# A new written order for the first tile of a linear-attention and gated-MLP kernel, on all engines

## The chip, the cores and the metric

The kernel runs on one core of a Trainium2 chip. The metric is the device time of one execution in microseconds. Five engines work in parallel, each through its own instructions in order: TensorE (PE in the profile, its weight loads PEld), VectorE (DVE), ScalarE (ACT), GpSimd (POOL) and SyncE (SP), which here issues all transfers.

## The reference

Inputs are r, k, v of shape (4, 8, 768, 48), a decay w and a bonus u per head and channel, and three MLP weights of 384x1536, 384x1536 and 1536x384, all float32.

```python
for t in range(S):
    cur = np.einsum('bhd,bhe->bhde', u[None] * kt, vt)
    y[:, :, t] = np.einsum('bhd,bhde->bhe', rt, state + cur)
    state = w[None, :, :, None] * state + np.einsum('bhd,bhe->bhde', kt, vt)
...
x = np.ascontiguousarray(attn_out.transpose(0, 2, 1, 3)).reshape(B * S, H * D)
gate = 1.0 / (1.0 + np.exp(-(x @ w_gate)))
val = x @ w_val
return (gate * val @ w_out).astype(np.float32)
```

## The kernel before, in words

The recurrence is computed in 12 chunks of 64 tokens; a chunk has two groups of heads, so there are 24 pieces n = 0, 1, 2, ... (a chunk's group 1 comes before its group 0). Two chunks make a tile of 512 tokens for the MLP; there are six tiles. The MLP's hidden width goes in 12 blocks f of 128. Every fp32 operand of the MLP is split into a high and a low part, and a product is three passes of matmuls (low weights by high x, high by high, high by low).

The first tile is special. The weights still have to be loaded and split while it runs, and its x comes chunk by chunk. So its MLP goes in 14 items i: blocks 0 and 1 for chunk 0 alone (256 columns, items 0 and 1), blocks 0 and 1 for chunk 1 (items 2 and 3), then blocks 2 to 11 for both (512 columns, items 4 to 13). All its work, with the attention of pieces 0 to 7 and part of 8 and 9, is written out by hand in the table START (line 42): 293 steps, run one after another by the loop behind `steps`; every step adds its instructions to the lists of the engines it uses, and each engine then works through its list in that order. Where a step's input isn't there, the engine waits, and everything behind it in its list waits too.

The letters of START that the prediction speaks of (n is a piece, f a block, i an item):

- L.n and X.n load a piece's channel-major tile (chan) and token-major tile (toks), W.f a block's weight words (wr, 1152 KB); all go through SyncE's one queue, in START's order. chan and toks have three buffers each. W.0's words lie in the buffer that W.11 needs.
- tk, ti, tp make the powers of the decay on VectorE; tp also copies them in turned order (line 184), tt transposes that on TensorE, tn writes the table tabn.
- A.n scales keys by the bonus (ScalarE, line 278); R.n scales the queries (line 284; on GpSimd, as Rv on VectorE); k.n scales the keys in place (VectorE, line 295); T.n scales the token-major keys (line 299; Tv on VectorE).
- Z.n makes the scores (TensorE, 64 matmuls, line 366), K.n keeps their causal part (VectorE, line 374), I.n applies them and, from n = 2 on, the state (line 328), O.n makes the outer products for the state. I.n takes two of the three PSUM banks named ring; they come free when h.n and l.n (high and low part of x, lines 465 and 469) and s.n (sum into the state; line 440 copies it for n = 0 and 1, line 438 adds) have read them. d.n decays the state (ScalarE, line 419).
- c.f, j.f, w.f, o.f rebuild and split a block's weights: scale (ScalarE, 232), three integer operations (VectorE, 238 to 240), high part (ScalarE, 246), low part (GpSimd, 249; ov on VectorE). Block 0 goes in two halves, c0, j0, w0, o0.
- U.i is the up product (18 matmuls into two ring banks, line 506), g.i sigmoid, m.i product, H.i and q.i high and low part of h (q on GpSimd, qv on VectorE, line 528), D.i the down product (9 matmuls, line 544). F.n copies x rows by small transfers (line 473).

Behind START a loop treats the other five tiles in a fixed pattern; U.14 is its first step.

Of the kernel before, what the change touches and what calls it, by code (L numbers as in the profile page):

```python
# [39 lines left out]


START = """
L.0 tc A.0 W.0 c0.1 X.1 tk ti.0 ti.1 tp L.1 W.1 Rv.0 k.0 c0.0 X.0 j0.1 Z.0 A.1 X.2 w0.1 j0.0 k.1
K.0 o0.1 I.0 W.2 tt w0.0 c.1 tn j.1 Tv.0 L.2 h.0 R.1 w.1 L.3 c.2 o.1 Tv.1 Z.1 l.0 K.1 A.2 O.0 W.5
s.0 I.1 k.2 O.1 R.2 F.0 X.3 s.1 h.1 A.3 Z.2 o0.0 W.3 X.4 l.1 L.4 K.2 W.7 T.2 U.0 R.3 g.0 k.3 I.2
O.2 c.3 W.4 Z.3 j.2 h.2 d.2 l.2 R.4 m.0 s.2 H.0 F.2 K.3 A.4 j.3 U.1 L.5 g.1 X.5 I.3 w.2 h.3 qv.0
d.3 T.4 T.3 w.3 D.0 k.4 O.3 l.3 R.5 s.3 m.1 Z.4 A.5 U.2 o.2 c.4 g.2 K.4 H.1 I.4 d.4 k.5 O.4 h.4 j.4
X.6 qv.1 Z.5 W.6 w.4 m.2 s.4 H.2 D.1 l.4 o.3 U.3 L.6 L.7 c.5 qv.2 D.2 W.11 g.3 K.5 F.4 o.4 A.6 m.3
j.5 H.3 Tv.5 U.4 g.4 R.6 qv.3 w.5 m.4 W.9 ov.5 F.1 I.5 O.5 H.4 D.3 d.5 h.5 k.6 Z.6 s.5 l.5 A.7 U.5
c.6 F.3 q.4 D.4 g.5 k.7 X.7 j.6 F.5 c.7 m.5 H.5 U.6 T.6 j.7 w.7 K.6 q.5 W.10 D.5 o.7 g.6 w.6 Rv.7  # L50
m.6 H.6 q.6 U.7 c.9 g.7 Z.7 ov.6 I.6 O.6 h.6 d.6 j.9 m.7 D.6 W.8 l.6 s.6 c.8 H.7 w.9 U.8 j.8 q.7
D.7 T.7 g.8 w.8 m.8 o.9 H.8 ov.8 q.8 U.9 g.9 D.8 K.7 U.10 c.10 m.9 c.11 H.9 j.10 g.10 I.7 q.9 m.10
O.7 H.10 h.7 l.7 d.7 w.10 D.9 q.10 s.7 ub L.8 X.8 Y.8 L.9 X.9 Y.9 U.11 D.10 g.11 j.11 m.11 o.10
U.12 F.6 H.11 w.11 g.12 ov.11 q.11 R.8 t.8 k.8 b.8 T.8 i.8 m.12 H.12 D.11 U.13 R.9 t.9 qv.12 k.9
g.13 m.13 H.13 Z.8 K.8 qv.13 b.9 T.9 i.9 D.12 F.7
"""


# [1 line left out]
def rwkv_then_moe(ctx: ExitStack, tc: tile.TileContext, wd, ub, ch, tk, rt, wt, rk0, vn0, wd0, out):  # L60
    nc = tc.nc
# [361 lines left out]

    def add_state(n):
        c, g = GROUPS[n]
        parts = [(0, 0, 0, 112)]
# [1 line left out]
        for s, to, lo, rows in parts:  # L430
# [444 lines left out]
```

## Time and profile before

| what | value |
|---|---|
| median of 3 runs | 558.22 us (557.37 to 559.66) |
| the profiled execution | 559.26 us |
| its span, first to last instruction | 557.5 us |
| TensorE busy | 521.9 us, 94% of the span |
| VectorE, ScalarE, GpSimd busy | 235.4, 184.1, 212.9 us |
| mean granted TensorE clock | 0.986 |

A profile gives busy time by engine, the engines' timelines with the idle time before each row and what ended it, and the same in windows. The clock is given as a share of its upper level: 1.00 is 2.4 GHz, 0.50 is 1.2 GHz. The idle time of an engine that nothing waits for costs nothing.

### The profile page before, as it was taken

The page shows a single profiled execution, that of the slowest core. Times are in us where ns is not written, and L with a number is a line of the kernel's source. Part 1 is how long each engine was busy: PE and PEld are TensorE (multiplying, and loading weights), DVE is VectorE, ACT ScalarE, POOL GpSimd, SP SyncE. Part 2 cuts the span into 40 slices and gives each one's busy share as a digit, 9 for nine tenths or more (in the row PEclk, how much of TensorE's full clock was granted, in tenths as well). Part 3 has the DMA queues.
Part 4 walks back from the last instruction along what each step waited for, and adds up shares of the span by engine and source line. Part 5 has one row for each costly group of instructions (what it writes and reads, how often), then busy time and mean ns, then how long its engine had stood idle before and what let it go on. Part 6 is the DMA issues. An engine that isn't in the chain of part 4 may idle for free. (4 is left out here: it accounts for less than half of the span.)

```text
span 557.5 us, 11987 instructions
## 1 busy us (share of the span) xinstructions
PE 521.9 (94%) x5204; PEld 427.1 (77%) x5204; DVE 235.4 (42%) x364; ACT 184.1 (33%) x394; POOL 212.9 (38%) x165
## 2 busy tenths in 40 slices
PE   1596899999999999999999999999999999999994
PEld 1486778777888888888888888888888888888883
DVE  7798799786524414324414324314324110101001
ACT  4466454633422322422322422322322221221111
POOL 3534234648254424254424254424234121111220
PEclk9998799999999999999999999999999999999998
DMA  8698911040221303221303221303220001100001
GB/s 329 265 364 311 368 36 54 30 111 2 88 83 52 92 16 86 79 77 67 92 15 88 77 80 65 93 13 89 78 75 5 11 1 19 58 0 1 0 1 61
DMA packets 15723, 47.84 MB, mean 86 GB/s; under 512 B 2384, under 2 KB 5200, under 8 KB 14256
## 3 DMA queue, kind: packets, MB, share of 16 engines
q1 hardware_dynamic: 15664, 47.01, 24.7%
q8 instruction: 43, 0.70, 0.5%
q14 instruction: 16, 0.13, 0.1%
HBM read 39.92 MB, written 4.72 MB: 80 GB/s over the span
## 5 line engine op out<-in xcount | busy, mean ns | idle before, releaser
L506 PE MATMUL ring<-xt,wx 128*128 128x512 f32 (+1 forms) x1332 | 317.8, 392 | 1.2 <-PE sc L366 0.8
L506 PEld LDWEIGHTS ring<-xt,wx 128*128 128x128 f32 x1332 | 248.2, 191 | 57.7 <-PE sc L366 0.9
L528 POOL TENSOR_TENSOR h<-sg,h 128x512 fp32r<-128x512 f32 x68 | 97.6, 1435 | 272.4 <-ACT h L524 272.4
L544 PE MATMUL acc<-h,wx 128*128 128x512 f32 (+1 forms) x666 | 164.6, 391 | 2.6 <-DVE h L528 1.3
L519 DVE TENSOR_TENSOR sg<-ring,sg 128x512 f32<-128x512 f32 (+1 forms) x74 | 50.0, 676 | 247.0 <-PE ring L506 247.0
L544 PEld LDWEIGHTS acc<-h,wx 128*128 128x128 f32 x666 | 122.4, 190 | 29.6 <-DVE h L528 1.5
L515 ACT ACTIVATE sg<-ring 128x512 f32<-128x512 f32 (+1 forms) x74 | 43.3, 586 | 158.9 <-PE ring L506 158.9
L524 ACT CAST h<-sg 128x512 fp32r<-128x512 f32 (+1 forms) x74 | 45.0, 608 | 150.6 <-DVE sg L519 150.6
L284 POOL TENSOR_TENSOR dec<-chan,tabk 128x512 f32<-128x512 f32 x22 | 30.7, 1397 | 12.4 <-ACT xt L465 6.9
L469 DVE TENSOR_TENSOR xt<-ring,xt 112x256 fp32r<-112x256 f32 (+1 forms) x52 | 20.0, 419 | 34.6 <-ACT xt L465 32.9
L249 POOL TENSOR_TENSOR wx<-wf,wx 128x1152 fp32r<-128x1152 f32 (+1 forms) x9 | 23.7, 2639 | 24.1 <-ACT wx L246 24.1
L295 DVE TENSOR_TENSOR chan<-chan,tabk 128x512 f32<-128x512 f32 x24 | 28.8, 1201 | 2.9 <-ACT dec L278 2.9
L366 PE MATMUL sc<-dec,chan 48*64 48x64 f32 x768 | 17.9, 236 | 12.2 <-DVE chan L295 10.2
L305 POOL TENSOR_TENSOR dec<-dec,toks 128x384 f32<-128x384 f32 x16 | 16.8, 1050 | 24.6 <-DMA dec<-in_rt 24.5
L366 PEld LDWEIGHTS sc<-dec,chan 48*64 48x64 f32 x768 | 15.3, 148 | 13.6 <-DVE chan L295 9.4
L299 POOL TENSOR_TENSOR toks<-toks,tabn 128x384 f32<-128x384 f32 x19 | 25.4, 1342 | 0.0
L374 DVE COPY_PREDICATED score<-masks,sc 128x512 f32<-128x512 int32 x32 | 23.9, 746 | 0.7
L328 PE MATMUL ring<-score,toks 64*48 64x64 f32 (+1 forms) x768 | 17.0, 226 | 7.5 <-DVE score L374 6.5
L419 ACT ACTIVATE state<-state,pw 112x96 f32<-112x96 f32 x80 | 23.4, 364 | 0.3 <-PE ring L328 0.2
L328 PEld LDWEIGHTS ring<-score,toks 64*48 64x48 f32 (+1 forms) x768 | 14.5, 134 | 8.6 <-issue 7.4
L240 DVE SCALAR_TENSOR_TENSOR wf<-wr,wf 128x1152 int32<-128x1152 int32 (+1 forms) x13 | 20.2, 1552 | 0.4
L239 DVE SCALAR_TENSOR_TENSOR wf<-wr,wf 128x1152 int32<-128x1152 int32 (+1 forms) x13 | 19.8, 1523 | 0.5
(61 smaller groups left out, 275.2 us busy)
## 6 DMA issues: line engine op xcount, KB each, us to landing
wr<-in_wt SPq DMA_DIRECT2D x11, 1152.0 KB, 11.9
chan<-in_ch SPq DMA_DIRECT2D x24, 512.0 KB, 4.0
toks<-in_tk SPq DMA_DIRECT2D x24, 400.0 KB, 4.4
out_y<-wf SPq DMA_DIRECT2D x17, 256.0 KB, 2.3
dec<-in_rt SPq DMA_DIRECT2D x16, 192.0 KB, 2.7
xt<-xt SPq DMA_DIRECT2D x30, 64.0 KB, 2.3
wr<-in_wt SPq DMA_DIRECT2D x2, 576.0 KB, 5.3
xt<-xt SPq DMA_DIRECT2D x12, 32.0 KB, 3.6
```

What stands on the lines that cost most here:

```text
L284: eng.tensor_tensor(v4(t[:, 0]), v4(chan[n][:, 0]), bc2(table_of(n)[:, :, ::-1]), ALU.mult)
L295: nc.vector.tensor_tensor(v4(k), v4(k), bc2(table_of(n)), ALU.mult)
L299: eng.tensor_tensor(v4(k), v4(k), bc2(tabn[:, 4 * g : 4 * g + 4]), ALU.mult)
L328: nc.tensor.matmul(yb[n][bank][64 * half : 64 * half + m, cs], lhsT, rhs, start=first, stop=stop, skip_group_check=True,)
L366: nc.tensor.matmul(sc[64 * gm : 64 * gm + 64, be, o : o + C], kk[row, cs : cs + C], rr[row, cs : cs + C], start=True, stop=True,)
L374: nc.vector.copy_predicated(t.rearrange("q (b m i) -> q b m i", b=2, m=4), masks[:, m].bitcast(I32).unsqueeze(1).unsqueeze(1).broadcast_to ...
L506: nc.tensor.matmul(o[:, self.cols], w[a][:, g * DM + kt * P : g * DM + (kt + 1) * P], self.x[:, kt, b, self.cols], start=(k == 0), stop=(k ...
L515: nc.scalar.activation(sg[:, c], self.pair[f][0][:, c], AF.Sigmoid)
L519: nc.vector.tensor_tensor(sg[:, c], self.pair.pop(f)[1][:, c], sg[:, c], ALU.mult)
L524: nc.scalar.copy(out=h[:, 0, c], in_=sg[:, c])
L528: eng.tensor_tensor(h[:, 1, c], self.sg.pop(f)[:, c], h[:, 0, c], ALU.subtract)
L544: nc.tensor.matmul(self.acc[d][:, self.cols], w[a][:, 2 * DM + d * P : 2 * DM + (d + 1) * P], h[:, b, self.cols], start=(f == 0 and k == 0 ...
```

## The change

START is written anew: the same products in another order on all engines, with some steps on another engine. Of the table's 13 lines the first stands here.

```diff
-L.0 tc A.0 W.0 c0.1 X.1 tk ti.0 ti.1 tp L.1 W.1 Rv.0 k.0 c0.0 X.0 j0.1 Z.0 A.1 X.2 w0.1 j0.0 k.1
+L.0 L.1 W.0 L.2 X.0 A.0 tc tk ti.1 tp ti.0 c0.0 k.0 Rv.1 j0.0 R.0 Z.0 trA tt c0.1 K.0 I.0 A.1 h.0
...
     def token_powers():
         power(32, 32, 32)
         power(64, 32, 64)
+
+    def token_order(copy):
         rev = turn[0] = hp.tile([P, 512], F32, name="sg").rearrange("q (p a j) -> q p a j", p=NP, a=2)
         pws = pw.rearrange("q (p s) j -> q p s j", p=NP)
-        nc.vector.tensor_copy(rev[0:64], pws[0:64, :, :, 95:31:-1])
+        copy(rev[0:64], pws[0:64, :, :, 95:31:-1])
         for gm in range(2):
-            nc.vector.tensor_copy(rev[64:128, :, gm], pws[64:128, :, 1 - gm, 95:31:-1])
+            copy(rev[64:128, :, gm], pws[64:128, :, 1 - gm, 95:31:-1])
...
-    def add_state(n):
+    def add_state(n, copy=nc.vector.tensor_copy):
...
             if c:
                 nc.vector.tensor_tensor(out, was, y, ALU.add)
             else:
-                nc.vector.tensor_copy(out, y)
+                copy(out, y)
...
+        "tr": lambda: token_order(nc.vector.tensor_copy), "trA": lambda: token_order(nc.scalar.copy),
+        "sa": lambda n: add_state(n, nc.scalar.copy), "tt": token_turn, "tn": token_table,
```

What the table changes by engine: trA and sa.0, sa.1 put seven copies on ScalarE. The low parts of the weights on VectorE go from four (blocks 5, 6, 8, 11) to six and a half (2, 4, 5, 6, 8, 9 and the first half of block 0). The low parts of h on VectorE go from six items to two (8 and 11). Rv goes from two pieces (0, 7) to five (1, 4, 7, 8, 9). The weights' order of loading goes from 0, 1, 2, 5, 3, 7, 4, 6, 11, 9, 10, 8 to 0, 1, 11, 3, 2, 5, 4, 7, 6, 9, 8, 10. In the changed kernel the lines from 184 on stand two further down, and those from 620 on three (the keys' scaling is line 297, the three integer operations 240 to 242).

First place: VectorE from the end of the decay's powers to the first kept scores, before the change (sg takes the turned powers, wf the weights, chan the keys, dec the queries).

```order
L184 COPY sg<-pw 64x512
L186 COPY sg<-pw 64x4x64 x2
L284 TENSOR_TENSOR dec<-chan,tabk 128x512
L295 TENSOR_TENSOR chan<-chan,tabk 128x512
L238 TENSOR_SCALAR wf<-wf 128x576
L239 SCALAR_TENSOR_TENSOR wf<-wr,wf 128x576
L240 SCALAR_TENSOR_TENSOR wf<-wr,wf 128x576
L238 TENSOR_SCALAR wf<-wf 128x576
L239 SCALAR_TENSOR_TENSOR wf<-wr,wf 128x576
L240 SCALAR_TENSOR_TENSOR wf<-wr,wf 128x576
L295 TENSOR_TENSOR chan<-chan,tabk 128x512
L374 COPY_PREDICATED score_97<-masks,sc 128x512 x2
```

The same stretch with the change:

```order
L175 RECIPROCAL tabk<-pw 128x4x32
L297 TENSOR_TENSOR chan<-chan,tabk 128x512
L286 TENSOR_TENSOR dec<-chan,tabk 128x512
L240 TENSOR_SCALAR wf<-wf 128x576
L241 SCALAR_TENSOR_TENSOR wf<-wr,wf 128x576
L242 SCALAR_TENSOR_TENSOR wf<-wr,wf 128x576
L376 COPY_PREDICATED score_97<-masks,sc 128x512 x2
L240 TENSOR_SCALAR wf<-wf 128x576
L241 SCALAR_TENSOR_TENSOR wf<-wr,wf 128x576
L242 SCALAR_TENSOR_TENSOR wf<-wr,wf 128x576
L297 TENSOR_TENSOR chan<-chan,tabk 128x512
```

The three copies are gone from VectorE, the first keys come ahead of the queries (which are now piece 1's), and K.0 stands ahead of block 0's second half and of k.1.

Second place: VectorE between K.2 and K.3, before the change (state and xt take what I.2 and O.2 left in the ring banks).

```order
L374 COPY_PREDICATED score_97<-masks,sc 128x512 x2
L295 TENSOR_TENSOR chan<-chan,tabk 128x512
L238 TENSOR_SCALAR wf<-wf 128x1152
L239 SCALAR_TENSOR_TENSOR wf<-wr,wf 128x1152
L240 SCALAR_TENSOR_TENSOR wf<-wr,wf 128x1152
L469 TENSOR_TENSOR xt<-ring,xt 112x2x128 x2
L519 TENSOR_TENSOR sg<-ring,sg 128x256
L438 TENSOR_TENSOR state<-state,ring 112x2x96 x2
L374 COPY_PREDICATED score_98<-masks,sc 128x512 x2
```

The same stretch with the change:

```order
L376 COPY_PREDICATED score_97<-masks,sc 128x512 x2
L240 TENSOR_SCALAR wf<-wf 128x1152
L241 SCALAR_TENSOR_TENSOR wf<-wr,wf 128x1152
L242 SCALAR_TENSOR_TENSOR wf<-wr,wf 128x1152
L297 TENSOR_TENSOR chan<-chan,tabk 128x512
L521 TENSOR_TENSOR sg<-ring,sg 128x256
L240 TENSOR_SCALAR wf<-wf 128x1152
L241 SCALAR_TENSOR_TENSOR wf<-wr,wf 128x1152
L242 SCALAR_TENSOR_TENSOR wf<-wr,wf 128x1152
L440 TENSOR_TENSOR state<-state,ring 112x2x96 x2
L471 TENSOR_TENSOR xt<-ring,xt 112x2x128 x2
L376 COPY_PREDICATED score_98<-masks,sc 128x512 x2
```

Two blocks of weights (3 and 2), not one, now stand between K.2 and the operations that free piece 2's ring banks.

Third place: SyncE's list from W.1 on, before the change (wr_156, wr_233, wr_320 are W.1, W.2, W.5; toks_161 is X.1).

```order
L226 DMA wr_156<-in_wt 128x1152
L107 DMA toks_161<-in_tk 128x800
L107 DMA toks_204<-in_tk 128x800
L226 DMA wr_233<-in_wt 128x1152
L102 DMA chan_248<-in_ch 128x1024
L102 DMA chan_256<-in_ch 128x1024
L226 DMA wr_320<-in_wt 128x1152
L473 DMA xt_250<-xt_250 16x2x256 x6
```

The same stretch with the change (wr_236, wr_247, wr_251 are W.1, W.11, W.3; toks_249 is X.1):

```order
L228 DMA wr_236<-in_wt 128x1152
L102 DMA chan_243<-in_ch 128x1024
L107 DMA toks_245<-in_tk 128x800
L228 DMA wr_247<-in_wt 128x1152
L107 DMA toks_249<-in_tk 128x800
L228 DMA wr_251<-in_wt 128x1152
L475 DMA xt_228<-xt_228 16x2x256 x6
L102 DMA chan_259<-in_ch 128x1024
```

W.11, whose buffer W.0's words hold until VectorE has joined both their halves, now stands third among the weights and ahead of X.1 and W.3.

## Rows read from the trace of the kernel before

**Rows 1.** The profile page, part 1: busy us (share), instructions.

```profile
PE 521.9 (94%) x5204; PEld 427.1 (77%) x5204; DVE 235.4 (42%) x364; ACT 184.1 (33%) x394; POOL 212.9 (38%) x165
```

**Rows 2.** Windows: stretch, us, busy of PE, PEld, DVE, ACT, POOL, clock, DMA share, GB/s.

```profile
9.39:29.98 20.59, 11.57 (x325) 10.32 (x325) 16.82 (x26) 9.92 (x21) 11.20 (x7) 1.00 0.76 298
29.98:48.34 18.36, 15.45 (x370) 13.82 (x366) 16.09 (x26) 12.29 (x32) 5.93 (x6) 0.91 0.86 313
48.34:65.73 17.39, 12.61 (x215) 11.97 (x215) 14.25 (x19) 8.28 (x18) 7.95 (x4) 0.80 1.02 421
65.73:102.00 36.27, 35.12 (x451) 28.64 (x450) 32.10 (x36) 19.47 (x36) 12.80 (x7) 1.00 0.23 71
102.00:138.69 36.69, 35.64 (x270) 28.37 (x269) 29.32 (x27) 15.38 (x27) 26.35 (x15) 1.00 0.16 43
138.69:557.50 418.81, 411.48 (x3584) 333.98 (x3582) 120.19 (x218) 114.63 (x254) 145.08 (x115) 0.99 0.17 52
```

**Rows 3.** Timeline of TensorE to U.0: start us, us, instructions [idle before <-releaser].

```profile
9.39 1.13 PE L366 MATMUL sc<-dec,chan 48*64 48x64 f32 x32 [9.39 <-DVE chan L295]
...
17.50 1.12 PE L328 MATMUL ring<-score,toks 64*64 64x64 f32 x32 [6.12 <-DVE score L374]
...
19.59 1.13 PE L366 MATMUL sc<-dec,chan 48*64 48x64 f32 x32
...
23.90 1.24 PE L328 MATMUL ring<-score,toks 64*64 64x64 f32 x29 [0.34 <-DVE score L374]
...
28.06 1.13 PE L366 MATMUL sc<-dec,chan 48*64 48x64 f32 x32 [1.98 <-POOL wx L249]
...
29.98 4.28 PE L506 MATMUL ring<-xt,wx 128*128 128x256 f32 x18
```

**Rows 4.** Timeline of ScalarE, its start.

```profile
0.75 1.28 ACT L136 ACT_TABLE_LOAD   x1 [0.75 <-PEq L860]
...
5.01 1.28 ACT L278 ACTIVATE dec<-chan,wu 128x128 f32<-128x128 f32 x4 [2.76 <-DMA chan<-in_ch]
7.99 1.35 ACT L232 ACTIVATE wf<-wr 128x576 f32<-128x576 f32 x2 [1.70 <-DMA wr<-in_wt]
```

**Rows 5.** Timeline of VectorE, single rows between 8 and 35 us.

```profile
8.65 0.69 DVE L295 TENSOR_TENSOR chan<-chan,tabk 128x512 f32<-128x512 f32 x1
...
12.49 1.83 DVE L240 SCALAR_TENSOR_TENSOR wf<-wr,wf 128x576 int32<-128x576 int32 x1
...
30.80 1.50 DVE L374 COPY_PREDICATED score<-masks,sc 128x512 f32<-128x512 int32 x2
...
32.79 0.75 DVE L238 TENSOR_SCALAR wf<-wf 128x1152 int32<-128x1152 int32 x1
33.57 1.36 DVE L239 SCALAR_TENSOR_TENSOR wf<-wr,wf 128x1152 int32<-128x1152 int32 x1
```

**Rows 6.** Timeline of TensorE from U.0 to U.4.

```profile
34.19 0.68 PE L328 MATMUL ring<-dec,state 48*64 48x64 f32 x32
...
37.78 2.40 PE L506 MATMUL ring<-xt,wx 128*128 128x256 f32 x18 [0.39 <-DVE sg L519]
...
58.28 0.70 PE L366 MATMUL sc<-chan,dec 48*64 48x64 f32 x16 [4.22 <-issue]
...
61.00 3.81 PE L506 MATMUL ring<-xt,wx 128*128 128x256 f32 x18
64.65 1.25 PE L544 MATMUL acc<-h,wx 128*128 128x256 f32 x9
```

**Rows 7.** Timeline of TensorE from U.4 to U.14, the two longest waits.

```profile
74.10 0.69 PE L366 MATMUL sc<-dec,chan 48*64 48x64 f32 x32 [0.83 <-DVE chan L295]
...
109.99 0.96 PE L544 MATMUL acc<-h,wx 128*128 128x512 f32 x3 [0.90 <-POOL h L528]
```

**Rows 8.** DMA queues: packets, MB, share; the page's part 3, then 53 to 59 us.

```profile
q8 instruction: 43, 0.70, 0.5%
...
q8 instruction: 1, 0.02, 1.0%
```

More of the change, by code (lines that the diff above doesn't have):

```diff
@@ L42 @@
 START = """
-L.0 tc A.0 W.0 c0.1 X.1 tk ti.0 ti.1 tp L.1 W.1 Rv.0 k.0 c0.0 X.0 j0.1 Z.0 A.1 X.2 w0.1 j0.0 k.1
[L44 to L53, printed above, removed]
@@ L54 @@
-U.12 F.6 H.11 w.11 g.12 ov.11 q.11 R.8 t.8 k.8 b.8 T.8 i.8 m.12 H.12 D.11 U.13 R.9 t.9 qv.12 k.9
-g.13 m.13 H.13 Z.8 K.8 qv.13 b.9 T.9 i.9 D.12 F.7
+L.0 L.1 W.0 L.2 X.0 A.0 tc tk ti.1 tp ti.0 c0.0 k.0 Rv.1 j0.0 R.0 Z.0 trA tt c0.1 K.0 I.0 A.1 h.0
+tn j0.1 k.1 W.1 R.2 T.0 l.0 L.3 X.2 W.11 X.1 W.3 F.4 F.0 L.4 X.4 W.2 W.5 X.3 c.1 Z.1 O.0 j.1 w0.1
+A.2 w0.0 k.2 o0v.0 K.1 Tv.1 I.1 Z.2 O.1 sa.0 w.1 h.1 l.1 Tv.2 K.2 c.3 sa.1 o.1 o0.1 R.3 U.0 g.0 A.3
+c.2 I.2 O.2 j.3 k.3 m.0 Z.3 d.2 A.4 h.2 H.0 w.3 j.2 U.1 g.1 s.2 l.2 F.5 L.6 X.5 L.5 F.2 W.4 X.7 W.7
@@ new lines @@
+X.6 L.7 K.3 q.0 T.3 T.4 I.3 O.3 d.3 h.3 w.2 k.4 Rv.4 m.1 s.3 l.3 Z.4 D.0 K.4 I.4 O.4 d.4 s.4 R.5
+U.2 U.3 h.4 l.4 A.5 H.1 g.2 g.3 c.4 k.5 ov.2 m.2 R.6 o.3 q.1 D.1 Z.5 U.4 m.3 c.5 A.6 H.3 H.2 g.4
+j.4 K.5 Tv.5 k.6 q.2 I.5 O.5 Z.6 m.4 j.5 A.7 k.7 Rv.7 d.5 h.5 w.4 l.5 s.5 q.3 D.2 D.3 H.4 ov.4 U.5
+W.6 L.8 L.9 W.9 q.4 W.8 F.3 W.10 F.1 D.4 U.6 g.5 w.5 k.8 m.5 c.6 H.5 ov.5 K.6 U.7 g.6 c.7 q.5 j.6
+m.6 Tv.6 j.7 g.7 w.6 H.6 w.7 Z.7 I.6 O.6 d.6 c.8 D.5 h.6 ov.6 m.7 U.8 o.7 U.9 g.8 K.7 s.6 l.6 q.6
+D.6 j.8 m.8 Rv.8 w.8 H.7 c.9 ov.8 T.7 j.9 q.7 U.10 g.9 H.8 c.10 qv.8 t.8 w.9 g.10 m.9 Z.8 I.7 O.7
@@ L56 @@
+D.7 D.8 j.10 k.9 h.7 w.10 H.9 m.10 ov.9 l.7 q.9 o.10 U.11 U.12 ub F.6 F.7 Y.9 X.9 Y.8 X.8 H.10 d.7
+c.11 s.7 g.11 j.11 m.11 q.10 w.11 o.11 D.9 D.10 g.12 m.12 H.12 H.11 U.13 Rv.9 b.8 i.8 qv.11 b.9 i.9
+q.12 T.8 D.11 D.12 g.13 t.9 m.13 K.8 H.13 q.13 T.9
 """
@@ L617, in rwkv_then_moe @@
         "tc": constants, "tk": channel_table, "ti": inverses, "tp": token_powers,
-        "tt": token_turn, "tn": token_table,
+        "tr": lambda: token_order(nc.vector.tensor_copy), "trA": lambda: token_order(nc.scalar.copy),
+        "sa": lambda n: add_state(n, nc.scalar.copy), "tt": token_turn, "tn": token_table,
         "c": lambda f: scale_words(f, ALL), "c0": lambda j: scale_words(0, HALVES[j]),
```

## The prediction

> **What bounds the kernel now.** The page's part 1 comes first: TensorE is busy for 94% of the span [rows 1]. All that another order can give back is TensorE's idle time and what it does at its lower clock, so the next question is where these lie. The windows answer it [rows 2]. From U.14 on, where the loop starts that the change doesn't touch, TensorE is busy for 411.48 of 418.81 us, and the 7.3 us missing belong to the end of the program. From 65.73 (the start of U.4) to 138.69 (U.14) it misses 72.96 - 35.12 - 35.64 = 2.2 us. Before 65.73 it misses 9.39 + 9.02 + 2.91 + 4.78 = 26.1 us, the first term being the time to its first matmul [rows 3], and the two stretches from U.0 to U.4 have a mean granted clock of 0.91 and 0.80, so part of them ran at 1.2 GHz. Third come the timelines, for who is waited for. Up to U.0 it is VectorE: the waits of 9.39 and 6.12 us end with it [rows 3], and it is busy for 16.82 of 20.59 us. From U.0 to U.4 the longest wait, 4.22 us, ends with "issue" [rows 6]: nothing that the profile records was waited for.
>
> TensorE's work up to U.14 is the same in both orders. So I write the start of U.14 as a sum over three stretches (to U.0, to U.4, to U.14) and carry the shift through to the end.
>
> **To U.0.** ScalarE's first scaling starts at 5.01, when the first keys land, and takes 1.28 [rows 4]. In the new list it comes ahead of the constants, so a table load stands before it and a second one, for the sigmoid, behind it. The first load of 1.28 [rows 4] starts once the keys are there: A.0 ends at 5.01 + 1.28 + 1.28 = 7.57. The second, and half of the 1.35 for block 0's first half, put the end of c0.0 at 7.57 + 1.28 + 0.2 + 0.68 = 9.7. The 0.2 is my allowance for the one-column activation between. VectorE's k.0 writes where A.0 reads: 7.57 + 0.69 [rows 5] gives Z.0 at 8.3, against 9.39 [rows 3]. On VectorE the three integer operations take 0.75 + 1.36 + 1.36 = 3.47 for a whole block (the third as long as the second) and some 1.9 for half of one; K takes 1.50 [rows 5]. I.0 then starts at 9.7 + 1.9 + 1.5 = 13.1, or up to 1.1 later: the operation at 12.49 took 1.83 for half a block [rows 5] because GpSimd was at work. Before it was 17.50 [rows 3]. Behind it j0.1 (1.9) and k.1 (0.7) give Z.1 at 15.7 to 16.8, against 19.59. Then l.0 (0.8), j.1 (3.5), k.2 (0.7), the low part of half of block 0 (0.7) and K.1 (1.5) make 7.2 (those without a row by their columns, from 0.69 for 512): I.1 at 22.9 to 24.0. There the lead is nearly spent, for it was 23.90 [rows 3]; VectorE now does the work between that formerly came behind I.1. But the 1.98 us before Z.2 go, since its keys are ready. I.1 and O.1 at 1.1 each [rows 3] and Z.2 at 1.9 (28.06 to 29.98, lower clock) end at 27.0 to 28.1, the four copies of h.1 need 1.5 more, the last of them beside U.0's first matmuls: U.0 at 28.8, 1.2 us earlier. I take 0 to 2.5 as the ends.
>
> In sentences of their own, for a page of the Trainium skill that speaks against this: "ScalarE: Activation LUTs", section "What ACT_TABLE_LOAD costs", says that a switch to another set costs about 1283 ns and a drain of about 1380 ns with it, 2.66 us in all. The trace agrees with the load's 1.28 and shows no switch between two sets. By the page c0.0 would end 1.4 us later, U.0 would come at 30.2, the term would be -0.2, and the forecast 552.2.
>
> The seven copies cost nothing. No row shows them on ScalarE; one lies between 0.32 (128 columns, a quarter of 1.28) and 0.68 (576 columns) [rows 4]. Three turned ones take 1.0 to 2.0, done by 11.7, and the transposes that read them stand ahead of I.0, which comes at 13.1 at the earliest. Were that cover gone, their excess would fall on I.0. The four state copies (1.3 to 2.7) fall into ScalarE's idle half (9.92 busy of 20.59 [rows 2]).
>
> **U.0 to U.4.** Before: 35.75 us, in which D.2's 1.08 (64.65 to 65.73 [rows 6]) stands; the new order has D.2 behind U.4, so 34.7 compare. The work in it: U.0 at 4.28 (lower clock [rows 3]), three up products at 2.40, two down products at 1.08, three groups of attention (I, O, Z) at 37.78 - 0.39 - 34.19 = 3.2 [rows 6]: 4.3 + 7.2 + 2.2 + 9.5 = 23.2. The other 11.5 are 2.91 + 4.78 of waiting [rows 2] and about 3.8 of lower clock: U.3 took 3.81, not 2.40, after the 4.22 us pause [rows 6], and so did its neighbours.
>
> What the new order makes of it. *Gone:* the pause. The instruction queue q8 moved 43 packets [rows 8]; TensorE has 2 x 5204 instructions [rows 1], 242 for each packet, so this is its own instruction stream. Around the pause the transfer engines were busy to 1.02 [rows 2], and one such packet lies in the window from 53 to 59 [rows 8]. I read it as a late fetch behind a queue of weights: a group of attention is 160 matmuls and as many loads in 3.2 us, so a packet lasts 2.4 us there. In the new order W.4 and W.7, the weights next due here, are issued only after the six small copies of F.2, and two up products (72 instructions in 4.8 us) follow I.4 and O.4, so a packet has time to come. With the pause its lower clock goes too. *New:* on VectorE, K.2 (1.5), j.3 (3.5), k.3 (0.7), m.0 (0.4), j.2 (3.5), s.2 and l.2 (1.4) run from about 29.8 on, so the ring banks of piece 2 come free at 40.8. TensorE reaches U.1's second bank at 33.0 (U.0 done) + 1.8 (I.2, O.2) + 1.0 (Z.3, after 0.7 to 1.0 of waiting for k.3) + 1.2 = 37.8: **a new wait of 3.0**, plus 1.0 for k.3. I.4 waits for K.4, which stands behind s.3 and l.3: 1.7. Behind such a wait the clock can fall, as after the pause; I take 1.0. Sum: 23.2 + 3.0 + 1.0 + 1.7 + 1.0 = 29.9; gain 34.7 - 29.9 = 4.8. Ends: 0.6 if a pause of 4.2 stays, 7.8 if the bank wait doesn't come.
>
> The work moved between VectorE and GpSimd is in these sums; outside them both have room (32.10 and 12.80 busy of 36.27 from U.4 on [rows 2]). W.11's 2.8 us of transfer (1152 KB at 421 GB/s) come before X.1: SyncE issues both once j0.1 is done (15.0 to 16.1); X.1 lands 2.8 + 1.0 (400 KB) and, as my estimate, 2 for starting later, at 21 to 22, ahead of I.1's 22.9.
>
> **U.4 to U.14.** 2.2 us are missing. The 0.83 before Z.6, for k.6, and the 0.90 inside D.8, for a low part from GpSimd [rows 7], belong to single late steps; k.6 now stands ahead of I.5, and D.8 behind U.10 with its low part on VectorE. I take 1.4 back, between 0 and 2.2. D.2's 1.08 has only moved here.
>
> **Sum.** 1.2 + 4.8 + 1.4 = 7.4 us. The profiled execution took 559.26, so 551.9; the median of the runs is 1.04 lower, 558.22, so **550.8 us**. A measurement of this kernel can tell some 0.5% (2.8 us) from no change. The ends add to 0.6 and 12.5; not all fall together, and I take 2.2 to 12.0: 546.2 to 556.0.
>
> **Rivals.**
> - *The pause of 4.2 us stays.* "Issue" names no cause, and the tie to the transfers rests on one case. Then 550.8 + 4.2 = 555.0. The Trainium skill, "Runtime: NRT & Kernel Launch", section "Instruction fetch mechanics", holds that fetching is sequential and mostly hidden; by that rule a busy transfer queue isn't the cause and the pause may come again. The row speaks against "hidden" here, not against the return.
> - *VectorE becomes the bound from 30 to 50 us.* Two blocks in a row ahead of s.2: each of six two-input operations can lose up to 1.1 to GpSimd as at 12.49 [rows 5], and block 3's words wait behind W.11 (2.8). If that adds 4.8 the second term is spent: 555.6, no change to tell. For it: 14.25 of 17.39 busy already [rows 2]. Against it: GpSimd has few steps there.
> - *Slower: the stream of instructions starves.* Between U.1 and U.2 the new order has I.3, O.3, Z.4, D.0, I.4, O.4, 530 instructions, over two packets; with one more before U.1 that can be three pauses: 550.8 + 12.7 = 563.5. It decides if weights fill the transfer queue at 40 to 50 us; at two pauses (559.2) it is even. Against it: only chan, toks and small copies are due there.
>
> **How the numbers follow.** The forecast's own case gets 0.68 (546.2 to 553.5 and a little past both), the pause that stays 0.12, VectorE as the bound 0.12, starving 0.08. Faster by over 0.5% means under 555.4: the first case and over half of the second, 0.75; the rest of the second with the third, 0.17; slower 0.08.
>
> **What would show it.** Right: first scores at 8.3, I.0 at 13 to 14, U.0 at 28.8, a wait of about 3 inside U.1, no "issue" wait over 1 us before U.4, U.3 at 2.4, U.4 near 58.7, U.14 near 131.3. Wrong: U.0 at 30 or later (VectorE's first stretch misread), an "issue" wait at 40 to 55 (the stream), a wait for weights' low parts in U.4 to U.9 (the new order of loading).

## The result and the profile after the change

The changed kernel took 551.48 us (median of 4 runs, 550.79 to 553.07), the kernel before beside it 557.86 (557.37 to 559.66): ratio 0.9884, with a 95% interval of 0.9852 to 0.9916. In a later series it came to 552.04 and 0.9885 (0.9856 to 0.9914). The forecast was 550.8. The profiled execution took 551.02 us, its span is 549.2.

The page's part 1 of the changed kernel answers to [rows 1]:

```profile
PE 517.2 (94%) x5204; PEld 423.8 (77%) x5204; DVE 225.5 (41%) x360; ACT 186.6 (34%) x402; POOL 197.3 (36%) x162
```

TensorE's busy time fell by 4.7 us for the same 5204 matmuls, and its mean granted clock rose from 0.986 to 0.994, so part of the gain is clock. The windows, with the columns of [rows 2], cut at the start of U.0, at 44.00 inside I.3, at U.4 and at U.14 (the first starts at 9.39 as before, though the first matmul now comes at 8.67):

```profile
9.39:29.36 19.97, 9.96 (x308) 8.89 (x303) 16.00 (x21) 11.18 (x27) 7.96 (x5) 1.00 0.87 327
29.36:44.00 14.64, 10.68 (x236) 9.55 (x240) 14.32 (x22) 9.48 (x24) 4.55 (x4) 1.00 0.79 303
44.00:59.41 15.41, 13.31 (x342) 12.57 (x340) 10.67 (x20) 9.88 (x25) 6.46 (x4) 0.89 0.82 321
59.41:131.03 71.62, 71.04 (x735) 58.04 (x728) 62.06 (x74) 37.89 (x69) 28.42 (x19) 1.00 0.30 106
131.03:549.20 418.17, 411.47 (x3584) 333.99 (x3582) 115.84 (x212) 114.02 (x253) 144.95 (x116) 1.00 0.17 52
```

VectorE is busy for 14.32 of the 14.64 us after U.0: there it bounds. From U.4 to U.14 TensorE now misses 0.6 us, before 2.2. The granted clock reads below 1.00 in one stretch only, the third. It reads 1.00 over U.0 too, in both kernels, though U.0's 18 matmuls took 4.28 us before and 0.80 + 3.67 here, against 2.40 for U.1 in [rows 6]; no row shows what slows them. The timeline of TensorE shows who is waited for:

```profile
8.67 1.14 PE L368 MATMUL sc<-dec,chan 48*64 48x64 f32 x32 [8.67 <-DVE chan L297]
...
14.37 1.12 PE L330 MATMUL ring<-score,toks 64*64 64x64 f32 x32 [2.08 <-DVE score L376]
16.94 1.13 PE L368 MATMUL sc<-dec,chan 48*64 48x64 f32 x32 [1.46 <-issue]
...
24.06 1.12 PE L330 MATMUL ring<-score,toks 64*64 64x64 f32 x32 [4.31 <-DVE score L376]
...
29.36 0.80 PE L508 MATMUL ring<-xt,wx 128*128 128x256 f32 x2 [1.65 <-ACT xt L467]
...
36.60 0.69 PE L368 MATMUL sc<-dec,chan 48*64 48x64 f32 x32 [0.64 <-DVE chan L297]
...
41.66 1.31 PE L508 MATMUL ring<-xt,wx 128*128 128x256 f32 x9 [2.64 <-DVE xt L471]
...
50.22 0.68 PE L330 MATMUL ring<-score,toks 64*64 64x64 f32 x32 [1.67 <-DVE score L376]
...
51.62 5.71 PE L508 MATMUL ring<-xt,wx 128*128 128x256 f32 x36
...
59.41 4.45 PE L508 MATMUL ring<-xt,wx 128*128 128x512 f32 x18
...
131.03 4.36 PE L508 MATMUL ring<-xt,wx 128*128 128x512 f32 x18
```

These are Z.0, I.0, Z.1, I.1, U.0, Z.3, the second half of U.1, the second part of I.4, U.2 with U.3, U.4 and U.14. They answer to [rows 3] and [rows 6]: the pause of 4.22 us that ended with "issue" is gone, and a wait of 2.64 for VectorE stands inside U.1.

Where the time came from, before minus after: to U.0 29.98 - 29.36 = 0.6; U.0 to U.4 (35.75 - 1.08 for D.2, which now lies behind) - 30.05 = 4.6; U.4 to U.14 (72.96 + 1.08) - 71.62 = 2.4; behind U.14 418.81 - 418.17 = 0.6. Together 8.3, the difference of the spans. The medians beside each other differ by 6.4, because executions of one kernel spread over some 3 us.

More places are needed below. VectorE's powers, its third integer operation for half of block 0, k.1, the last integer operation of j.2, and l.2, which frees the ring bank that U.1 waits for:

```profile
5.41 1.75 DVE L159 TENSOR_TENSOR pw<-pw 128x256 f32<-128x256 f32 x2
...
11.21 1.72 DVE L242 SCALAR_TENSOR_TENSOR wf<-wr,wf 128x576 int32<-128x576 int32 x1
...
16.16 0.68 DVE L297 TENSOR_TENSOR chan<-chan,tabk 128x512 f32<-128x512 f32 x1
...
38.89 1.77 DVE L242 SCALAR_TENSOR_TENSOR wf<-wr,wf 128x1152 int32<-128x1152 int32 x1
...
41.10 0.74 DVE L471 TENSOR_TENSOR xt<-ring,xt 112x256 fp32r<-112x256 f32 x2
```

GpSimd's R.0 and R.2 beside the first two:

```profile
5.58 1.31 POOL L286 TENSOR_TENSOR dec<-chan,tabk 128x512 f32<-128x512 f32 x1 [1.09 <-DVE tabk L175]
...
10.91 1.40 POOL L286 TENSOR_TENSOR dec<-chan,tabk 128x512 f32<-128x512 f32 x1 [4.03 <-PE sc L368]
```

And ScalarE's two table loads, from A.0 to c0.0:

```profile
6.48 1.28 ACT L280 ACTIVATE dec<-chan,wu 128x128 f32<-128x128 f32 x4
7.78 1.28 ACT L136 ACT_TABLE_LOAD   x1
9.07 0.20 ACT L136 ACTIVATE table<-spare 128x1 f32<-128x1 f32 x1
9.18 0.71 ACT L234 ACTIVATE wf<-wr 128x576 f32<-128x576 f32 x1
```

### The profile page after: what moved, and what is told of

It is laid out like the page before. It is cut to its first block, busy times and chain, and to the rows that moved or that the text cites. A ratio compares the mean times of both kernels' runs of the same rounds, so it can differ in the third digit from the quotient of the medians.

```text
span 549.2 us, 12001 instructions
## 1 busy us (share of the span) xinstructions
PE 517.2 (94%) x5204; PEld 423.8 (77%) x5204; DVE 225.5 (41%) x360; ACT 186.6 (34%) x402; POOL 197.3 (36%) x162
## 5 line engine op out<-in xcount | busy, mean ns | idle before, releaser
L530 POOL TENSOR_TENSOR h<-sg,h 128x512 fp32r<-128x512 f32 (+1 forms) x72 | 98.2, 1364 | 282.9 <-ACT h L526 282.9
L546 PE MATMUL acc<-h,wx 128*128 128x512 f32 (+1 forms) x666 | 161.8, 388 | 0.4 <-POOLq L700 0.4
L286 POOL TENSOR_TENSOR dec<-chan,tabk 128x512 f32<-128x512 f32 x19 | 25.2, 1328 | 9.5 <-PE sc L368 4.0
L301 POOL TENSOR_TENSOR toks<-toks,tabn 128x384 f32<-128x384 f32 x18 | 22.5, 1254 | 4.4 <-ACT tabn L199 4.4
L297 DVE TENSOR_TENSOR chan<-chan,tabk 128x512 f32<-128x512 f32 x24 | 21.6, 902 | 0.7 <-issue 0.7
L251 POOL TENSOR_TENSOR wx<-wf,wx 128x1152 fp32r<-128x1152 f32 (+1 forms) x6 | 15.0, 2505 | 19.2 <-ACT wx L248 19.2
L467 ACT CAST xt<-ring 112x256 fp32r<-112x256 f32 (+1 forms) x52 | 16.7, 364 | 13.5 <-PE ring L330 10.7
L440 DVE TENSOR_TENSOR state<-state,ring 48x192 f32<-48x192 f32 (+1 forms) x52 | 18.0, 350 | 6.5 <-ACT state L421 2.3
```

The costliest lines, as they stand in the source:

```text
L286: eng.tensor_tensor(v4(t[:, 0]), v4(chan[n][:, 0]), bc2(table_of(n)[:, :, ::-1]), ALU.mult)
L301: eng.tensor_tensor(v4(k), v4(k), bc2(tabn[:, 4 * g : 4 * g + 4]), ALU.mult)
L530: eng.tensor_tensor(h[:, 1, c], self.sg.pop(f)[:, c], h[:, 0, c], ALU.subtract)
L546: nc.tensor.matmul(self.acc[d][:, self.cols], w[a][:, 2 * DM + d * P : 2 * DM + (d + 1) * P], h[:, b, self.cols], start=(f == 0 and k == 0 ...
```

## Experiments

Each is timed against the kernel before on the same chip; a ratio carries its 95% interval. In the names, b_ is the kernel before with an edit, a_ the changed kernel with one.

### Is the pause a late fetch? The old order with the weights issued later (b_weights_late)

```diff
- ... U.3 L.6 L.7 c.5 ... W.11 ... W.9 ... X.7 ... W.10 ... W.8 ... ub L.8
+ ... U.3 L.6 L.7 X.7 L.8 W.11 W.9 W.10 W.8 c.5 ... ub
```

> The kernel before with its instructions unchanged on TensorE, VectorE, ScalarE and GpSimd; only SyncE's list differs: X.7 and L.8 come ahead of W.11, W.9, W.10, W.8, which so are issued from about 59 us on and not at 49.1 to 54.7. My theory (the 4.22 us of 'issue' before Z.5 are an instruction fetch that is late behind weight transfers): no 'issue' wait over 1 us from 50 to 60 us, U.3 at 2.4 us and not 3.81, U.4 at 59 to 61 and not 65.73, 551 to 553 us, ratio 0.988 to 0.991. Rival (the pause belongs to TensorE's own list, whatever is transferred): the pause stays between 3.5 and 4.5 us, U.4 at 65.2 to 66.2, ratio 0.998 to 1.002. In between (the chip's transfers of the six weights share the blame with something else): a pause of 1 to 3 us.

Measured 556.81 us, ratio 0.9966 (0.9945 to 0.9988). TensorE's timeline: the last part of Z.5, U.4, Z.6, U.5.

```profile
55.98 0.79 PE L366 MATMUL sc<-chan,dec 48*64 48x64 f32 x31
...
61.92 4.35 PE L506 MATMUL ring<-xt,wx 128*128 128x512 f32 x18
...
71.20 0.69 PE L366 MATMUL sc<-dec,chan 48*64 48x64 f32 x32 [1.75 <-DVE chan L295]
...
72.29 5.99 PE L506 MATMUL ring<-xt,wx 128*128 128x512 f32 x18
```

The pause is gone from the middle of Z.5 (in [rows 6] 16 of its 32 matmuls stand behind it), and U.4 comes 3.8 us earlier, though only SyncE's list has changed. That speaks for the fetch, but TensorE also came to the place later than before: I.4 waited 1.94 us for ScalarE (0.40 before), and the granted clock was 0.50 from 52.3 to 55.7 us. The table at the end of the section on a full transfer queue has the fetch itself. The time fell by 1.9 us, not by 5 to 7: Z.6 then waits 1.75 us for VectorE's k.6 (0.83 in [rows 7]), and U.5, behind that wait, takes 5.99 instead of 4.45.

### Keeping what the pause gave (b_weights_late_k6)

```diff
- ... Tv.5 U.4 g.4 R.6 qv.3 w.5 m.4 ... ov.5 ... k.6 Z.6
+ ... Tv.5 k.6 U.4 g.4 R.6 qv.3 w.5 m.4 ... ov.5 ... Z.6
```

> b_weights_late (the kernel before with W.11, W.9, W.10, W.8 issued late) with one step more moved: k.6 on VectorE from behind ov.5 to behind Tv.5, ahead of qv.3, m.4 and ov.5. Theory (the pause's end was worth 3.8 us at U.4, of which VectorE's order took back 0.9 as a longer wait for k.6 before Z.6, and the lower clock behind that wait 1.5 in U.5): Z.6 waits under 0.3, U.5 takes 4.4 and not 5.99, U.14 at 133.8 to 134.8 (137.0 to 137.3 in b_weights_late, 138.69 before), 553 to 554.5 us, ratio 0.990 to 0.993. Rival (the low parts behind k.6, now later, hold U.5 or U.6 in its place, or the pause shows up elsewhere): U.14 at 136 to 137.5, ratio 0.995 to 0.998.

Measured 556.85 us, ratio 0.9960 (0.9942 to 0.9978). TensorE's timeline, the second half of Z.5, and U.5:

```profile
56.13 0.46 PE L366 MATMUL sc<-chan,dec 48*64 48x64 f32 x16 [1.46 <-issue]
...
70.00 4.44 PE L506 MATMUL ring<-xt,wx 128*128 128x512 f32 x18
```

In the profiled execution the mechanism is the theory's: no wait for k.6, U.5 at the full clock, U.14 at 134.97 (138.69 before). In the same execution a pause of 1.46 us stands where 4.22 stood, so later weights shorten the pause and don't end it by themselves. The medians don't show the step's worth: 556.85 against 556.81. The theory on k.6 is not confirmed in time.

### Does a full transfer queue starve the new order? (a_weights_early, a_weights_five)

```diff
- ... L.5 F.2 W.4 X.7 W.7 X.6 L.7 ... W.6 ... W.9 ... W.8 ... W.10
+ ... L.5 W.4 W.7 W.6 F.2 X.7 W.9 X.6 L.7 W.8 W.10 ...
```

> The changed kernel, all lists unchanged but SyncE's: W.4, W.7, W.6 come ahead of F.2 (issued at about 38.5 to 40 us, not 45.8 to 53) and W.9, W.8, W.10 behind them without a wait, so that the transfer engines are full from 39 to about 57 us, over I.3, O.3, Z.4, I.4, O.4. My theory (a burst of attention under a full transfer queue starves TensorE's instructions): one or more 'issue' waits of 2 to 4 us between 43 and 60 us, U.4 at 61.5 to 64 and not 59.41, 553.5 to 557 us. Rival (the new order of TensorE's list ended the pause, transfers play no part): no 'issue' wait over 0.5 us, U.4 at 59.0 to 59.8, 551 to 552 us. A wait for F.2's rows ahead of U.2 would be named 'DMA xt' and stand apart from both.

Measured 553.37 us, ratio 0.9905 (0.9873 to 0.9937): no "issue" wait over 0.3 us from U.0 to U.4, a wait of 1.54 us for F.2's rows before U.2, U.4 at 60.89. To fill the queue over the whole burst, five were put ahead of F.2:

```diff
- ... L.5 F.2 W.4 X.7 W.7 X.6 L.7 ... W.6 ... W.9 ... W.8
+ ... L.5 W.4 W.7 W.6 W.9 W.8 F.2 X.7 X.6 L.7 ...
```

> The changed kernel, all lists unchanged but SyncE's: W.4, W.7, W.6, W.9, W.8 ahead of F.2, so that 5.8 MB queue up at 38 to 40 us and keep the transfer engines full to about 52 us, over I.3, O.3, Z.4, D.0, I.4 and O.4 (a_weights_early had three weights, full to about 48, and showed no pause). Theory (an instruction packet queues behind the weights issued before it, and TensorE pauses only where what it has fetched ahead runs out before that backlog does): one 'issue' wait of 1.5 to 4 us between 46 and 53 us, ahead of U.2. Rival (the pause of the kernel before had another cause, transfers do nothing to the fetch): no 'issue' wait over 0.5 us. Both: F.2's rows come behind the weights, so U.2 waits for 'DMA xt' to 54 to 57 us, and the time is 554 to 558 us; the verdict is read from the kind of the wait, not from the time.

Measured 560.06 us, ratio 1.0032 (1.0014 to 1.0051). U.2 in TensorE's timeline:

```profile
58.93 6.91 PE L508 MATMUL ring<-xt,wx 128*128 128x256 f32 x36 [6.33 <-DMA xt<-xt]
```

The window from 40 to 52 us (columns as in [rows 2]):

```profile
40.00:52.00 12.00, 9.33 (x246) 8.61 (x250) 7.56 (x16) 4.97 (x13) 4.87 (x5) 0.72 1.01 415
```

The transfer engines were busy to 1.01 over I.3 to O.4, and no "issue" wait from U.0 to U.4 passed 0.3 us: the new order had no pause under a full queue either. What the weights did do is hold back F.2's small copies, for which U.2 waited 6.33 us. That wait weakens the test, since TensorE stood still while an instruction packet could come.

The traces hold the packets of the instruction queue q8 one by one. In the old order the pause stands behind the same matmul each time, the 851st of the program (in the middle of Z.5's second half); in the new order the 851st stands in Z.5's first half. Times in us:

| run | packet | 851st starts | 852nd starts |
|---|---|---|---|
| the kernel before | 56.00 to 56.92 | 53.85 | 58.28 |
| b_copies (below) | 57.09 to 58.02 | 54.91 | 59.55 |
| b_weights_late | 53.74 to 54.94 | 56.21 | 56.31 |
| b_weights_late_k6 | 53.84 to 54.77 | 54.45 | 56.13 |
| the changed kernel | 53.65 to 54.58 | 58.66 | 58.67 |
| a_weights_early | 52.50 to 53.60 | 60.13 | 60.14 |
| a_weights_five | 54.94 to 56.14 | 67.18 | 67.19 |

In all four rows of the old order the 852nd matmul starts 1.36 to 1.53 us behind the packet's end, b_weights_late's too. So the pause is a wait for that packet. With the weights later the packet ended some 2 us earlier than in the kernel before, which is half of the pause; in b_weights_late the other half went because TensorE came 2.4 us later. In the new order TensorE reaches the place 4.1 us or more behind the packet's end, because U.2 and U.3 (5.71 us in the changed kernel) now stand ahead of Z.5. So neither run with early weights could show a late packet at this place. That the packet serves the same place in the new order is read from the count, not shown.

### The copies on VectorE again, and on ScalarE in the old order (a_copies_back, b_copies)

```diff
- ... Z.0 trA tt ... sa.0 ... sa.1
+ ... Z.0 tr tt ... s.0 ... s.1
```

> The changed kernel with its seven copies put back on VectorE, at the same places of the table (the turned powers between block 0's first half and K.0, the state copies of pieces 0 and 1 ahead of l.0's and l.1's followers). Theory (VectorE is who is waited for up to U.0, the copies lie on its path): three copies of 1.0 us together move K.0 and I.0 to 15.3 to 15.6 (14.37 with the change), U.0 to 30.3 to 31.0 (29.36), 552 to 553.3 us. Rival (the copies on ScalarE delay the transposes by 0.51 and gain nothing, since I.1 waits for something else): U.0 at 29.0 to 29.6, 551.0 to 551.8 us.

Measured 556.07 us, ratio 0.9944 (0.9923 to 0.9966), 3.3 us slower than the changed kernel by the ratios. TensorE at I.1 and U.0:

```profile
24.84 0.47 PE L330 MATMUL ring<-score,toks 64*64 64x64 f32 x2 [4.35 <-DVE score L376]
26.77 1.00 PE L330 MATMUL ring<-score,toks 64*64 64x64 f32 x27 [1.46 <-DVE state L442]
...
32.05 0.80 PE L508 MATMUL ring<-xt,wx 128*128 128x256 f32 x2 [1.63 <-ACT xt L467]
```

U.0 comes at 32.05, 2.7 us later than in the first profile of the changed kernel, more than the theory's 0.9 to 1.6. It counted the turned copies only; the state copy on VectorE stands behind K.1 and T.1, and I.1 waits 1.46 us for the bank that it frees.

```diff
- ... k.0 c0.0 X.0 ... s.0 ... s.1
+ ... k.0 c0.0 trA X.0 ... sa.0 ... sa.1
```

> The kernel before in its own order with only the seven copies put on ScalarE (the turned powers behind c0.0, the state copies where s.0 and s.1 stood). Theory (VectorE's chain to K.0 gets shorter by the copies' 0.92 and I.1 and U.0 no longer meet a state copy; but Z.2 waits for GpSimd's low part, which follows from block 0's joined words): K.0 and I.0 0.8 to 1.0 earlier (I.0 16.5 to 16.8 and not 17.50), U.0 0.5 to 1.2 earlier at 28.8 to 29.5, the pause before Z.5 stays, 557.0 to 558.0 us, ratio 0.997 to 0.999. Rival (the copies are worth the 2.9 us at U.0 that putting them back cost the changed kernel): U.0 at 27.0 to 28.0, 555 to 556.5 us, ratio 0.994 to 0.996. Rival 2 (no gain, the waits move): U.0 at 29.8 to 30.2, ratio 0.999 to 1.001.

Measured 559.34 us, ratio 1.0013 (0.9996 to 1.0029): no difference. TensorE at I.1 and in the middle of Z.5:

```profile
26.12 1.01 PE L330 MATMUL ring<-score,toks 64*64 64x64 f32 x27 [3.10 <-ACT state L442]
...
59.55 0.71 PE L368 MATMUL sc<-chan,dec 48*64 48x64 f32 x16 [4.42 <-issue]
```

ScalarE's list, c.2 and the state copy:

```profile
23.45 1.24 ACT L234 ACTIVATE wf<-wr 128x1152 f32<-128x1152 f32 x1 [2.74 <-POOL wx L251]
...
25.77 0.51 ACT L442 COPY state<-ring 112x192 f32<-112x192 f32 x2
```

I.0 comes at 16.15 instead of 17.50. Then the gain is lost: the state copy stands behind c.2, which waits 2.74 us for GpSimd's low part, and I.1 waits 3.10 us for it. The pause in Z.5 stays, with the weights where they were. The copies pay only in an order in which nothing that waits stands ahead of them.

### Is the new wait in U.1 the loss? (a_j2_later)

```diff
- ... w.3 j.2 U.1 ... s.2 l.2 ... K.3 q.0
+ ... w.3 U.1 ... s.2 l.2 ... K.3 j.2 q.0
```

> The changed kernel with j.2 behind K.3 on VectorE, so that s.2 and l.2 free piece 2's ring banks 3.5 to 4 us earlier. Theory (VectorE's work is the bound from 30 to 58 us; a wait removed in U.1 comes again where TensorE next needs VectorE): the wait of 2.64 us inside U.1 goes, Z.4 or I.4 then wait 3 to 5 us for k.4 and K.4, U.4 at 59.0 to 60.5, 551 to 553 us. Rival (the bank wait is the loss itself): U.4 at 56.8 to 57.6, U.14 at 128.4 to 129.2, 548.5 to 549.5 us.

Measured 554.27 us, ratio 0.9932 (0.9908 to 0.9955). TensorE at Z.4:

```profile
47.12 1.13 PE L368 MATMUL sc<-dec,chan 48*64 48x64 f32 x32 [4.49 <-issue]
```

VectorE's last operation of j.2, and Rv.4:

```profile
43.51 2.30 DVE L242 SCALAR_TENSOR_TENSOR wf<-wr,wf 128x1152 int32<-128x1152 int32 x1
...
46.34 0.68 DVE L286 TENSOR_TENSOR dec<-chan,tabk 128x512 f32<-128x512 f32 x1
```

The theory held in kind, though U.4 at 60.73 and the time lie past its ends (60.5 and 553). The wait of 2.64 shrank to 0.25, and 4.49 us came before Z.4. The row calls them "issue", but Rv.4, whose queries Z.4 reads, ended at 47.02 and Z.4 began at 47.12: this is a wait for VectorE. VectorE's work bounds the stretch, and moving a block only moves the wait.

### The second table load (a_tc_first)

```diff
- L.0 L.1 W.0 L.2 X.0 A.0 tc tk ...
+ L.0 L.1 W.0 L.2 X.0 tc A.0 tk ...
```

> The changed kernel with the constants ahead of A.0, as in the kernel before, so that ScalarE loads its table once, before the keys land. Theory (VectorE's powers set Z.0, the second table load only c0.0): A.0 ends 1.28 earlier, at 6.5; k.0 and Z.0 stay at 7.9 and 8.7, c0.0 ends at 7.3 to 8.0 and not 9.89, VectorE's first integer operation comes at 9.1 to 9.3 and not 9.92, I.0 at 13.6 to 14.0, U.0 at 28.3 to 29.0, 550.4 to 551.2 us. Rival 1 (a switch between two tables costs 2.66 us and not 1.28): c0.0 ends at 6.5 to 7.2 and the gain is the same, since VectorE then bounds. Rival 2 (I.1 and h.1's copies are bound by transfers, not by the start): U.0 at 29.2 to 29.6, no gain.

Measured 551.78 us, ratio 0.9858 (0.9826 to 0.9889). ScalarE's c0.0, now without a load ahead of it:

```profile
7.56 0.72 ACT L234 ACTIVATE wf<-wr 128x576 f32<-128x576 f32 x1 [1.39 <-DMA wr<-in_wt]
```

TensorE at I.1 and U.0:

```profile
25.58 1.12 PE L330 MATMUL ring<-score,toks 64*64 64x64 f32 x32 [7.58 <-DMA toks<-in_tk]
...
30.86 0.80 PE L508 MATMUL ring<-xt,wx 128*128 128x256 f32 x2 [1.63 <-ACT xt L467]
```

c0.0 began 1.62 us earlier and K.1 1.73 earlier (20.79 for 22.52), but I.1 then waited for X.1, and U.0 came later, at 30.86. Rival 2 held in kind (U.0 lies past its 29.6): X.1's landing lay close behind VectorE's chain. The profiled execution was the slowest of the five (552.79), so the others may have lost less. Why X.1, issued at 14.9, took until some 25.4 to land no run settles.

### Low parts back on GpSimd (a_low_parts_back)

```diff
- ... o0v.0 ... ov.2 ... ov.4 ... ov.9
+ ... o0.0 ... o.2 ... o.4 ... o.9
```

> The changed kernel with four low parts of weights back on GpSimd (blocks 2, 4, 9 and the first half of block 0), which leaves three on VectorE (5, 6, 8). Theory (their move to VectorE is not what shortened the stretch from U.4 to U.14; that came from k.6 ahead of I.5 and D.8 behind U.10): U.4 to U.14 at 71.4 to 72.1 (71.62 with the change), U.4 at 58.7 to 60.0, 551 to 552.5 us, ratio 0.986 to 0.990. Rival (GpSimd, at 2.6 to 2.7 us for a low part and slowed by VectorE, holds U.4 or U.6): a wait for 'POOL wx' of 1 to 3 us there, U.14 at 132.5 to 134.5, 553 to 555 us, ratio 0.990 to 0.995.

Measured 554.86 us, ratio 0.9932 (0.9911 to 0.9953). VectorE's Rv.7:

```profile
70.20 3.17 DVE L286 TENSOR_TENSOR dec<-chan,tabk 128x512 f32<-128x512 f32 x1
```

GpSimd's o.4:

```profile
70.08 2.74 POOL L251 TENSOR_TENSOR wx<-wf,wx 128x1152 fp32r<-128x1152 f32 x1 [5.62 <-ACT wx L248]
```

TensorE in U.5:

```profile
74.44 2.33 PE L508 MATMUL ring<-xt,wx 128*128 128x512 f32 x9 [1.68 <-DVE state L440]
```

U.4 to U.14 took 134.68 - 60.94 = 73.7 us, not 71.6; in the profiles of the eight other kernels and runs named a_ it took 71.5 to 71.6. The theory fell, and the rival had the size but not the place: nothing waited for GpSimd's result. Its 2.74 us held VectorE's next two-input operation for 3.17 instead of 0.69, l.5 and s.5 came late behind it, and U.5 waited for their bank.

### A version that combines two edits (a_tc_x1), and the changed kernel beside it

```diff
- ... X.0 A.0 tc ... W.1 ... L.3 X.2 W.11 X.1 W.3
+ ... X.0 tc A.0 ... W.1 X.1 X.2 ... L.3 W.11 W.3
```

> The changed kernel with the constants ahead of A.0 (as in a_tc_first) and with X.1 and X.2 issued behind W.1, ahead of L.3, W.11 and W.3. Theory (up to U.0 two bounds stand close together: VectorE's chain, which a_tc_first moved 1.73 us earlier, and X.1's landing, which W.11 ahead of it set): X.1 lands before 18, T.1 follows K.1 at 22.1 to 22.4 without a wait, I.1 at 22.2 to 22.5, U.0 at 27.4 to 28.0, U.4 at 57.4 to 58.4, 549.0 to 550.5 us. Rival 1 (the transfer engines are full to 24 us whatever the order, so another load comes late, W.1 or W.3, and U.0 stays): U.0 at 29.0 to 30.9, 551 to 553 us. Rival 2 (VectorE's work from 30 to 50 us takes the gain back): U.0 at 27.4 to 28.0 but U.4 at 59.0 to 59.8, 551 to 552 us.

Measured 550.39 us, ratio 0.9862 (0.9837 to 0.9887): U.0 at 27.62, as the theory and rival 2 had it, but U.4 at 58.87, nearer to rival 2, and the time within the theory's. Both kernels once more, on one chip:

> The changed kernel itself once more, beside a_tc_x1_again on the same chip, to tell the two apart. Both theories: U.0 at 29.2 to 29.5, U.4 at 59.2 to 60.5, 551.0 to 553.0 us, ratio 0.985 to 0.990.

> a_tc_x1 once more (constants ahead of A.0, X.1 and X.2 ahead of L.3, W.11, W.3). Theory (the 1.74 us won at U.0 shrink to about 0.5 at U.4, because VectorE's K.4 and the lower clock take the rest): 0.3 to 1.5 us under a_again, 549.8 to 551.5 us. Rival (all of it is taken back): within 0.3 us of a_again.

Measured 552.04 us for the changed kernel (0.9885, 0.9856 to 0.9914) and 549.41 for this version (0.9840, 0.9817 to 0.9863). It was lower both times, by 1.1 and 2.6 us (0.3 to 1.5 were expected of the second); the intervals still touch, and the two profiled executions took the same time (549.60 and 549.63), so a gain over the changed kernel is likely and not settled. TensorE of a_tc_x1_again, U.0 and U.4:

```profile
27.59 0.80 PE L508 MATMUL ring<-xt,wx 128*128 128x256 f32 x2 [1.65 <-ACT xt L467]
...
57.59 4.45 PE L508 MATMUL ring<-xt,wx 128*128 128x512 f32 x18
```

In a_again U.0 came at 28.16, which the expectation (29.2 to 29.5) missed. U.0, and VectorE's third integer operation in that execution:

```profile
28.16 0.80 PE L508 MATMUL ring<-xt,wx 128*128 128x256 f32 x2 [1.65 <-ACT xt L467]
...
10.90 0.76 DVE L242 SCALAR_TENSOR_TENSOR wf<-wr,wf 128x576 int32<-128x576 int32 x1
```

and GpSimd's R.2:

```profile
10.91 1.88 POOL L286 TENSOR_TENSOR dec<-chan,tabk 128x512 f32<-128x512 f32 x1 [4.03 <-ACT sg L188]
```

Here VectorE was 0.01 us ahead, took 0.76, and GpSimd waited. In the first profile it came at 11.21, behind R.2's 10.91, and took 1.72. The same kernel's I.0 lies at 13.14 or 14.37, and U.0 moves with it.

## Why the prediction was right, and where it was not

The time and the range held, and so did the sum: 7.4 us forecast up to U.14, 7.7 in the first profile, 9.1 in a_again's (U.14 at 129.58). That the total came so near in the first is in part luck: the three terms missed by -0.6, -0.2 and +1.0. Of the signs, one fails by its letter: an "issue" wait of 1.46 us stands before U.4, ahead of Z.1. It is VectorE's k.1, which ended at 16.84; Z.1 began at 16.94. Step by step:

- **To U.0: 1.2 forecast; 0.6 in one execution, 1.8 in another.** Z.0 came at 8.67, not 8.3, because VectorE's powers and not A.0 ended last: they took 1.75 beside GpSimd's R.0. I.0's "up to 1.1 later" was the right allowance; who comes first there decides it. The Trainium skill, "SBUF — State Buffer", section "SBUF: two separate sides", says that of a two-input VectorE operation and a GpSimd operation whichever starts first holds the shared ports to its end. The rows at 10.90 and 11.21 agree, with 0.76 and 1.72. X.1's landing at 21 to 22 "ahead of I.1" was too bold: a_tc_first had it at about 25.4, and it was a bound nearly as late as VectorE. The "lower clock" that the forecast gives Z.2 and U.0 is not in the rows: the granted clock reads 1.00 from 9.39 to 40 us. Their times stand in both kernels alike, so the sum doesn't hang on it.
- **The table loads.** The forecast counted 1.28 for the switch. A.0 ended at 7.76, the load ran from 7.78 to 9.06, the next activation began at 9.07: 1.28, and no drain in the rows. The Trainium skill, "ScalarE: Activation LUTs", section "What ACT_TABLE_LOAD costs", has 2.66 for a switch; the trace doesn't agree, so the 552.2 us by that figure had no ground here.
- **The copies "cost nothing".** True, and under-read: they were taken as cover for ScalarE's idle time and given no worth of their own. Taken back they cost 3.3 us; alone in the old order they gave nothing.
- **U.0 to U.4: 4.8 forecast, 4.6 measured.** The new bank wait was 2.64 (3.0 forecast), k.3 0.64 (1.0), K.4 1.67 (1.7), the lower clock about 1.2 (1.0): U.2 with U.3 took 5.71, not 4.80, and O.4 0.97, not 0.64. (The sum writes three groups of 3.2 as 9.5, which moves it by 0.1.) The rival of VectorE as the bound was half right: all these waits end with it, and a_j2_later shows that they only move. They were already in the sum, which is why the rival's extra 4.8 didn't come.
- **Why the pause went.** The late fetch is shown for the old order: in four profiles, three of them with a pause, the 852nd matmul starts 1.36 to 1.53 us behind the end of an instruction packet. "Behind a queue of weights" is half of it: later weights brought the packet some 2 us earlier, and 1.46 us of pause were left in b_weights_late_k6. What else sets the packet's time is open. Of the two reasons given for the pause's absence in the new order, the second is borne out by the rows: two up products now stand ahead of Z.5, and the place comes 4.1 us behind the packet's end. No run isolates it. The first, weights issued later, was not needed: with them early again there was no pause, but there TensorE came later still. The Trainium skill, "Runtime: NRT & Kernel Launch", section "Instruction fetch mechanics", has fetching mostly hidden. The trace agrees in the new order and not in the old one, where TensorE stood for 4.22 us.
- **U.4 to U.14: 1.4 forecast, 2.4 measured.** This is the mis-sized term, past its own upper end of 2.2. The waits of 0.83 and 0.90 went, as forecast, and of the 2.4 some 1.6 are idle time (2.2 to 0.6); the other 0.8 is TensorE's busy time, which no run explains. The work moved between VectorE and GpSimd was said to have "room" on both outside the other terms; a_low_parts_back shows that four of those moves alone are worth 2.1 us there, because a GpSimd operation of 2.74 us held a two-input VectorE operation for most of its length.
- **The slower rival**, three pauses in the stream of 530 instructions, did not come, not even under a full transfer queue; that the wait of 1.67 us for VectorE inside the stream gave the packets time is only argued.

## What to carry to other kernels

Where one engine bounds a stretch, sum its work before moving a step within it: the wait that is removed comes back at the next place. A pause marked "issue" in the middle of a group of matmuls whose inputs and bank were all there has no data to wait for: look for the instruction queue's packet just before its end. The same word ahead of a group can hide another engine's operation, so look there for the one that ended just before. Moving an operation to an idle engine pays only if nothing that waits stands ahead of it there.
